# Second expert pass by seven products: the last sums of a chunk issued among the next chunk's products, a plain last chunk, three conversion steps per product

## The chip, the core and the metric

One NeuronCore of a Trainium2 chip runs the whole program. The metric is device time in microseconds (us) of one execution. The engines are TensorE (PE in the profile, PEld for its weight loads), VectorE (DVE), ScalarE (ACT), GpSimd (POOL) and the queue on SyncE (SP) that issues most transfers. Each engine takes its instructions in the order in which they were issued to it.

## What is computed

Attention with a decay mask on 4 x 8 heads of 576 positions, then two feed-forward layers on the 2304 tokens, all in float32:

```
ret = scores * Dmat            # scores = q k^T / sqrt(64), Dmat the decay mask
x   = ret @ v                  # as 2304 tokens x 512
r   = relu(x @ w_in);  x = (r * r) @ w_out                  # 512 -> 2048 -> 512
out = sum_e p[:, e] * (relu(x @ w1[e]) @ w2[e])             # 4 experts, 512 -> 1024 -> 512
```

## The kernel before

Every float32 operand of a product is split into a high part, rounded to the matmul's float32r format, and a low part, the rest; a product is then three matmuls (high by high, high by low, low by high) that add up in one PSUM bank. In the helper `split` (L129 to L131) ACT writes the high part and POOL subtracts it from the source for the low part.

The hidden width of both feed-forward layers is cut into chunks of 256: chunks 0 to 7 belong to the first layer, 8 to 23 to the four experts, and 24 to 39 are the experts' chunks once more. The tokens lie in five groups (four of 512, one of 256). Chunks 8 to 23, the first expert pass, serve groups 0, 1 and 4; chunks 24 to 39, the second expert pass, serve groups 2 and 3. The first pass converts the experts' weights (`split_w1`, `split_w2`: splits, and sums of weight blocks on DVE) in small steps. `tick(n)` issues the next n steps from a list, after every product of the pass; how many is in `pace`. `drain` issues what is left at once, where a chunk's weights must be ready. `keep` writes converted weights to DRAM after some empty steps, and `fetch` reads them back in the second pass through the SP queue, into one of two buffers per weight.

The second pass works on 2 x 2 blocks by Winograd's form of Strassen's scheme, in both layers: seven block products in place of eight, with sums of blocks around them. `first_layer(c)` is a generator with seven steps. Each issues one product of six matmuls (L791) into a PSUM bank and its sums: ACT copies the first bank to `u0` (L810), DVE adds (L798) and applies relu and the expert's probability (L801), POOL subtracts (L804). The results are seven operands for the second layer, each split by `operand`: "21", "22", "t3", "11", "t1", "t2", "t4". The last three are built on sums of the others: t1 = b12 - b11, t2 = b22 - t1, t4 = t2 - b21; all sources lie in the `spare_xh`/`spare_xl` tiles, t3 in a `wraw` tile. `second_layer(c)` takes the operands in the order 22, 21, t3, 11, t1, t2, t4: each step is two products of three matmuls (L860), and `gather` (L866 to L870) adds each bank to one of eight running sums e1 to e4, on DVE, or for the first chunk copies it there on ACT (L868). The main loop (from L1025) puts the steps of `first_layer(c)` and `second_layer(c - 1)` by turns, so a chunk is seven steps of twelve matmuls, 84 in all, for chunks 25 to 39. Order within each engine is the order of this code. The fourth step of `first_layer` adds a second product to the bank of the first, which `u0` must have been copied from by then.

The second layer of chunk 39 runs alone after the loop (`unit`, `second_layer(39)`): the last three operands are made there too, and as sums become final DVE combines them to the four output blocks (L904 to L906), `put` scales them by a stored factor on POOL, the last two on DVE (L933), and SP sends them out (L935).

Of the kernel before, what the change touches and what calls it, by code (L numbers as in the profile page):

```python
# [6 lines left out]
F32 = mybir.dt.float32  # L7
# [26 lines left out]
def tile_kernel(ctx, tc, qT, kT, kn, vn, v4d, mask, qdec, kdec, wd, w, probs, probs2, out, outT):  # L34
# [170 lines left out]
    def keep(f, c):  # L205

        for _ in range(3):
            yield
        for i, t in enumerate(w1t[c] if f is split_w1 else w2t[c]):
            d = dram.tile([128, 8 * BC], F32, name=f"kept{int(f is split_w2)}_{c}_{i}")  # L210
            nc.sync.dma_start(out=d, in_=f32(t))
            kept[f, c, i] = d

    def fetch(f, c):

        names = ("w2hi", "w2lo") if f is split_w2 else ("w1hi", "w1lo")
        parts = ((0, 1), (2, 8)) if f is split_w2 else ((0, 3), (4, 8))
        t = [wp.tile([128, 8 * BC], F32R, name=n) for n in names]
        for a, b in parts:
            for i in range(2):  # L220
                p = slice(BC * a, BC * b)
                nc.sync.dma_start(out=f32(t[i][:, p]), in_=kept[f, c - NW2, i][:, p])
        if f is split_w2:
            w2t[c] = t
        else:
            w1s[c] = [x.rearrange("p (i k m) -> p i k m", i=8, k=2) for x in t]
# [267 lines left out]
    with tc.manual_schedule():  # L494
# [260 lines left out]
        spare = []  # L755
        taken, ops, prow, sums = [0], {}, [], []

# [15 lines left out]
        def first_layer(c):  # L773
# [29 lines left out]
            def minus(o, x, y):  # L803
                g.tensor_tensor(out=o, in0=x, in1=y, op=ALU.subtract)  # L804
# [15 lines left out]
            product(b1, A12, 4, False)  # L820
            relu(b12, b1, 0)
            yield
            b5 = bank()
# [8 lines left out]
            o["22"] = operand(b22)  # L832
            minus(t3, b22, b12)
            o["t3"] = operand(t3)
            yield
# [3 lines left out]
            o["11"] = operand(b11)  # L839
            minus(b12, b12, b11)  # L840
            o["t1"] = operand(b12)
            minus(b22, b22, b12)
            o["t2"] = operand(b22)
            minus(b21, b22, b21)
            o["t4"] = operand(b21)
            yield

        def second_layer(c):
# [3 lines left out]
            o = ops.pop(c)  # L852
            first, last = c == NW1 + NW2, c == NW - 1
            bank = lambda: [ps.tile([128, GT], F32, name="h", tag="ps") for _ in range(2)]
# [11 lines left out]
            def gather(e, b, op=ALU.add, first=first):  # L866
                if first:
                    nc.scalar.copy(out=e, in_=b)  # L868
                else:
                    v.tensor_tensor(out=e, in0=e, in1=b, op=op)  # L870

            e1, e2, e3, e4 = ([t[:, 2 * i + d, :] for d in range(2)] for t in sums for i in range(2))
            bb = bank()
# [13 lines left out]
            for d in range(2):  # L887
                product(ba[d], H11, "11", False)
                gather(e1[d], ba[d])
                if last:  # L890
                    put(e1[d], 1, 0, d)
            yield
# [6 lines left out]
            for d in range(2):  # L899
                product(be[d], R2, "t2")  # L900
                gather(e2[d], be[d], first=False)
                if last:
                    c12, c22 = e2[d], e3[d]
                    v.tensor_tensor(out=c12, in0=e1[d], in1=e2[d], op=ALU.add)  # L904
                    v.tensor_tensor(out=c22, in0=c12, in1=e3[d], op=ALU.subtract)
                    v.tensor_tensor(out=e4[d], in0=c22, in1=e4[d], op=ALU.subtract)  # L906
                    put(c12, 0, 0, d)
                    put(c22, 0, 1, d)
            yield
            for d in range(2):  # L910
                product(bc[d], H22, "t4", False)
                if last:
                    v.tensor_tensor(out=e4[d], in0=e4[d], in1=bc[d], op=ALU.subtract)
                    put(e4[d], 1, 1, d, v)
                else:
                    gather(e4[d], bc[d])
            yield

        back = []

        def unit():
# [7 lines left out]
        def put(c, g, half, d, engine=nc.gpsimd):  # L929

            o = spare[put.n % 8] if engine is nc.gpsimd else c
            put.n += 1
            engine.tensor_tensor(out=o, in0=c, in1=back[g], op=ALU.mult)  # L933
            r = 256 * half + 128 * d
            nc.sync.dma_start(out=outT[r : r + 128, GT * g : GT * g + GT], in_=o)  # L935

        put.n = 0

# [25 lines left out]
        for i, job in enumerate(jobs):  # L964
# [4 lines left out]

            pace[0] = 4 if i < 3 else 3 if c in (p, q) else 4 if c == z else 2  # L970
            if job == (NW1, (0, 1)):
# [132 lines left out]
```

## Time and profile before

| | |
|---|---|
| median of 3 runs | 1382.35 us (1379.69 to 1383.57) |
| the profiled execution | 1382.66 us |
| its span, first to last instruction | 1380.9 us |
| PE busy | 1246.1 us, 90% |
| DVE, POOL, ACT busy | 901.4, 684.4, 442.9 us |
| mean granted TensorE clock | 0.952 of full speed |

The profile is one execution. Busy time is what an engine spent in instructions; matmuls overlap (a 128 x 512 matmul is shown with 0.39 us and the next starts 0.23 us after it), so the pace of PE is read from starts. The granted clock is 1.0 at 2.4 GHz and 0.5 at 1.2 GHz. By the timeline, the first pass of experts ends at about 918 us, the products of chunk 24 alone run to 939.81 us, the loop over chunks 25 to 39 to 1351.80 us, and the rest is the last second layer and the outputs.

### The profile page before, as it was taken

How to read it: one execution, taken by the hardware profiler on the slowest of the kernel's cores; microseconds unless marked ns; L12 is line 12 of the kernel's file. 1: busy time of each engine (PE TensorE's matmuls, PEld its weight loads, DVE VectorE, ACT ScalarE, POOL GpSimd, SP SyncE). 2: the span in 40 equal slices, each digit the busy share in tenths (PEclk: the TensorE clock that was granted, in tenths of full speed). 3: DMA queues.
4: the chain of work that ended last, by engine and by line, in shares of the span. 5: the costliest groups of instructions: out<-in, count | busy, mean ns of one | idle time of the engine just before them, and what ended most of it. 6: DMA issues, size and time to landing. Idle time of an engine off the chain costs nothing.

```text
span 1380.9 us, 18028 instructions
## 1 busy us (share of the span) xinstructions
PE 1246.1 (90%) x6464; PEld 1033.0 (75%) x6464; DVE 901.4 (65%) x1520; ACT 442.9 (32%) x1047; POOL 684.4 (50%) x702
## 2 busy tenths in 40 slices
PE   7999999999999999999999999877777887888684
PEld 6888888888888788878878788666656665666563
DVE  4776777877786846777767676754545554565457
ACT  4546333333333443433333333412111111111111
POOL 5655454545452535444543454504554465455547
PEclk9999999999999999999999999998898898899888
DMA  9911111111110144554545355564343344324421
GB/s 345 295 33 54 46 46 47 47 46 46 47 54 0 77 153 170 219 212 161 229 181 201 152 225 218 221 245 159 130 163 133 107 149 171 107 107 158 161 69 61
DMA packets 61277, 188.04 MB, mean 136 GB/s; under 512 B 7682, under 2 KB 12802, under 8 KB 52996
## 3 DMA queue, kind: packets, MB, share of 16 engines
q1 hardware_dynamic: 60676, 186.19, 37.3%
q8 instruction: 51, 0.84, 0.3%
q10 hardware_dynamic: 512, 0.70, 0.1%
q14 instruction: 38, 0.31, 0.1%
HBM read 115.02 MB, written 71.85 MB: 135 GB/s over the span
## 4 chain that ended last, share of the span: by engine, by line
PE 68%; POOL 15%; DVE 7%; ACT 5%; issue 3%; DMA 2%; SPq 0%; ACTq 0%; POOLq 0%; DVEq 0%
PE h L545 16%; PE o L740 14%; PE o L709 13%; PE h L579 11%; PE h L791 7%; PE h L860 5%; POOL glo L131 4%; POOL ghi L131 4%; POOL spare_xh L804 3%; POOL wraw L804 2%; ACT ghi L130 1%; POOL spare_xl L804 1%; ACT glo L130 1%; DVE xl L668 1%; PE qk L346 1%
## 5 line engine op out<-in xcount | busy, mean ns | idle before, releaser
L791 PE MATMUL h<-xh,w1hi 128*128 128x512 f32 x224 | 100.6, 449 | 83.0 <-ACT r L810 68.2
L131 POOL TENSOR_TENSOR glo<-r,ghi 128x512 fp32r<-128x512 f32 (+1 forms) x80 | 96.9, 1212 | 153.5 <-ACT ghi L130 143.3
L870 DVE TENSOR_TENSOR sums<-sums,h 128x512 f32<-128x512 f32 x214 | 139.6, 682 | 24.6 <-PE h L860 24.6
L545 PE MATMUL h<-xh,w1hi 128*128 128x512 f32 (+1 forms) x448 | 154.2, 344 | 0.8 <-DVE xl L433 0.8
L545 PE MATMUL h<-xl,w1hi 128*128 128x512 f32 (+1 forms) x448 | 154.1, 344 | 0.0
L545 PE MATMUL h<-xh,w1lo 128*128 128x512 f32 (+1 forms) x448 | 154.1, 344 | 0.0
L131 POOL TENSOR_TENSOR w2lo<-wraw,w2hi 128x256 fp32r<-128x256 f32 x64 | 52.2, 837 | 163.9 <-ACT w2hi L130 163.9
L740 PE MATMUL o<-w2lo,ghi 128*128 128x512 f32 x320 | 126.6, 395 | 4.5 <-POOL w2lo L131 4.5
L740 PE MATMUL o<-w2hi,ghi 128*128 128x512 f32 x320 | 126.5, 395 | 4.1 <-DVE oacc L748 3.0
L740 PE MATMUL o<-w2hi,glo 128*128 128x512 f32 x320 | 126.4, 395 | 0.0
L791 PEld LDWEIGHTS h<-xh,w1hi 128*128 128x128 f32 x224 | 47.8, 213 | 99.3 <-ACT r L810 73.6
L709 PE MATMUL o<-glo,w2hi 128*128 128x512 f32 (+1 forms) x320 | 118.2, 369 | 1.0 <-POOL glo L131 1.0
L709 PE MATMUL o<-ghi,w2hi 128*128 128x512 f32 (+1 forms) x320 | 118.0, 369 | 0.0
L709 PE MATMUL o<-ghi,w2lo 128*128 128x512 f32 (+1 forms) x320 | 117.8, 368 | 0.0
L748 DVE SCALAR_TENSOR_TENSOR oacc<-o,pr,oacc 128x512 f32<-128x512 f32 x150 | 107.6, 742 | 10.3 <-PE o L740 10.3
L798 DVE TENSOR_TENSOR r<-h,r 128x512 f32<-128x512 f32 x16 | 11.1, 692 | 153.3 <-ACT r L810 151.2
L550 DVE TENSOR_TENSOR r<-r 128x512 f32<-128x512 f32 (+1 forms) x80 | 62.4, 779 | 65.4 <-ACT r L549 65.1
L791 PE MATMUL h<-xl,w1hi 128*128 128x512 f32 x224 | 95.7, 427 | 0.0
L791 PE MATMUL h<-xh,w1lo 128*128 128x512 f32 x224 | 94.9, 424 | 0.0
L579 PE MATMUL h<-xh,w1hi 128*128 128x512 f32 x224 | 88.2, 394 | 6.6 <-ACT w1hi L130 5.0
L545 PEld LDWEIGHTS h<-xh,w1hi 128*128 128x128 f32 x448 | 84.9, 189 | 11.6 <-DVE xl L433 0.9
L545 PEld LDWEIGHTS h<-xl,w1hi 128*128 128x128 f32 x448 | 84.9, 189 | 10.6
(157 smaller groups left out, 3056.8 us busy)
## 6 DMA issues: line engine op xcount, KB each, us to landing
wraw<-wd SPq DMA_DIRECT2D x64, 256.0 KB, 2.8
wraw<-w SPq DMA_DIRECT2D x64, 256.0 KB, 3.0
kept<-w1hi SPq DMA_DIRECT2D x16, 1024.0 KB, 5.2
kept<-w1lo SPq DMA_DIRECT2D x16, 1024.0 KB, 7.1
kept<-w2hi SPq DMA_DIRECT2D x16, 1024.0 KB, 5.4
kept<-w2lo SPq DMA_DIRECT2D x16, 1024.0 KB, 6.3
w2hi<-kept SPq DMA_DIRECT2D x16, 768.0 KB, 5.1
w2lo<-kept SPq DMA_DIRECT2D x16, 768.0 KB, 6.2
```

The costliest lines, as they stand in the source:

```text
L130: nc.scalar.copy(out=hi, in_=src)
L131: nc.gpsimd.tensor_tensor(out=lo, in0=src, in1=f32(hi), op=ALU.subtract)
L545: nc.tensor.matmul(h, wk(a, f, k), group(x, g, k), start=(n == 0), stop=(n == 3 * KT - 1))
L550: nc.vector.tensor_tensor(out=r, in0=r, in1=r, op=ALU.mult)
L579: nc.tensor.matmul(o, a[:, i, k, :], slot(x, j)[:, k, :], start=(first and n == 0), stop=(n == 5), skip_group_check=True,)
L709: nc.tensor.matmul(o, a[:, f, 128 * m : 128 * m + 128], x[:, f, :], start=(n == 0), stop=(n == 3 * FT - 1))
L740: nc.tensor.matmul(o, a[:, f, 128 * m : 128 * m + 128], x[:, f, :], start=(n == 0), stop=(n == 3 * FT - 1))
L748: nc.vector.scalar_tensor_tensor(out=acc, in0=o, scalar=pr[:, tt, e : e + 1], in1=acc, op0=ALU.mult, op1=ALU.add)
L791: nc.tensor.matmul(o, a[:, i, k, :], slot(x, j)[:, k, :], start=(first and n == 0), stop=(n == 5), skip_group_check=True,)
L804: g.tensor_tensor(out=o, in0=x, in1=y, op=ALU.subtract)
L860: nc.tensor.matmul(b, a[:, BC * i + 128 * d : BC * i + 128 * d + 128], o[x][:, y, :], start=(first and n == 0), stop=(n == 2), skip_group_ ...
L870: v.tensor_tensor(out=e, in0=e, in1=b, op=op)
```

## The change

It has four parts.

1. In `first_layer` the operands t1, t2, t4 and the sums between them are no longer issued in the seventh step but put as four functions on a list `later`; the main loop takes one after each step of `first_layer`, before the step of `second_layer`. The seventh step fills the list before it yields, so the first function is issued at the end of that step and the other three in steps 1 to 3 of the next chunk.
2. The last chunk uses no seven products in its second layer: it makes operands "12", "21", "22", "11" alone, and `outputs` replaces `unit`, `put` and `second_layer(39)`. POOL combines the sums e1 to e4 to the four output blocks in six subtractions or additions, beside that 8 outputs of six matmuls are made, and DVE adds each to its block and scales it. Of the last w2, `fetch` reads the first four blocks alone.
3. `gather` copies the first chunk's banks on DVE, not on ACT.
4. `pace` is 3 rather than 2 in the first expert pass (4 in its last chunk as before), and `keep` waits one step rather than three.

```diff
     def keep(f, c):
-        for _ in range(3):
-            yield
+        yield
...
-        parts = ((0, 1), (2, 8)) if f is split_w2 else ((0, 3), (4, 8))
+        parts = ((0, 3), (4, 8))
+        if f is split_w2:
+            parts = ((0, 1), (2, 8)) if c < NW - 1 else ((0, 4),)
...
             relu(b12, b1, 0)
+            if c == NW - 1:
+                o["12"] = operand(b12)
...
-            minus(t3, b22, b12)
-            o["t3"] = operand(t3)
+            if c < NW - 1:
+                minus(t3, b22, b12)
+                o["t3"] = operand(t3)
...
             o["11"] = operand(b11)
-            minus(b12, b12, b11)
-            o["t1"] = operand(b12)
-            minus(b22, b22, b12)
-            o["t2"] = operand(b22)
-            minus(b21, b22, b21)
-            o["t4"] = operand(b21)
+            def one():
+                o["t1"] = operand(b12)
+                minus(b22, b22, b12)
+            def two():
+                o["t2"] = operand(b22)
+            def three():
+                minus(b21, b22, b21)
+            def four():
+                o["t4"] = operand(b21)
+            if c < NW - 1:
+                minus(b12, b12, b11)
+                later.extend((one, two, three, four))
             yield
...
                 if first:
-                    nc.scalar.copy(out=e, in_=b)
+                    v.tensor_copy(out=e, in_=b)
...
+        def outputs(c):
...
+            for a, b, op in ((e2, e1, ALU.add), (e3, e2, ALU.subtract), (e4, e3, ALU.subtract)):
+                for d in range(2):
+                    x, y = (a, b) if op == ALU.add else (b, a)
+                    nc.gpsimd.tensor_tensor(out=a[d], in0=x[d], in1=y[d], op=op)
+            for e, half, g, xs in (
+                (e1, 0, 1, ("11", "21")), (e2, 0, 0, ("12", "22")), (e3, 1, 0, ("12", "22")), (e4, 1, 1, ("11", "21"))
+            ):
+                for d in range(2):
...
+                    v.tensor_tensor(out=e[d], in0=e[d], in1=b, op=ALU.add)
+                    v.scalar_tensor_tensor(
+                        out=e[d], in0=e[d], scalar=1.0, in1=back[g], op0=ALU.mult, op1=ALU.mult
+                    )
+                    r = 256 * half + 128 * d
+                    nc.sync.dma_start(out=outT[r : r + 128, GT * g : GT * g + GT], in_=e[d])
...
-            pace[0] = 4 if i < 3 else 3 if c in (p, q) else 4 if c == z else 2
+            pace[0] = 4 if i < 3 else 3 if c in (p, q) else 4 if c == z else 3 if c >= NW1 else 2
...
-            for _ in zip(first_layer(c), second_layer(c - 1)):
-                pass
+            f, t = first_layer(c), second_layer(c - 1)
+            for _ in f:
+                if later:
+                    later.pop(0)()
+                next(t)
             queue_weights((split_w1, c + 2), (split_w2, c + 1))
-        unit()
-        for _ in second_layer(NW - 1):
-            pass
+        outputs(NW - 1)
```

On ACT, this is one chunk of the second pass before, from the copy of its first bank to that of the next chunk's. The first four casts are the high parts of 21, 22, t3 and 11, the next three those of t1, t2 and t4.

```order
L810 COPY r<-h 128x512
L130 CAST ghi<-spare_xh_9145 128x512
L130 CAST glo<-spare_xl_9146 128x512
L130 CAST ghi<-wraw 128x512
L130 CAST glo<-spare_xl_9146 128x512
L130 CAST ghi<-spare_xh_9145 128x512
L130 CAST glo<-spare_xl_9146 128x512
L130 CAST ghi<-spare_xh_9145 128x512
L810 COPY r<-h 128x512
```

And a chunk in the same tiles on ACT in the changed kernel, from the cast of 21 to that of t4:

```order
L130 CAST ghi<-spare_xh_9145 128x512
L130 CAST glo<-spare_xl_9146 128x512
L130 CAST ghi<-wraw 128x512
L130 CAST glo<-spare_xl_9146 128x512
L130 CAST ghi<-spare_xh_9145 128x512
L811 COPY r<-h 128x512
L130 CAST glo<-spare_xl_9146 128x512
L130 CAST ghi<-spare_xh_9145 128x512
```

The next chunk's copy has moved up past the casts of t2 and t4, and still stands behind the cast of t1. On POOL, DVE and PE the order within such a chunk is what it was.

On ACT ahead of chunk 23's first layer, the last chunk of the first pass, before (w1hi and w2hi are high parts of converted weights, L592 is ACT's copy of the first bank of a chunk, and the chunk's first product reads the first w1hi blocks):

```order
L130 CAST w2hi<-cv_d 128x256
L130 CAST w1hi<-wraw 128x256
L130 CAST w1hi<-cv_d 128x256
L130 CAST w1hi<-cv_m 128x256
L130 CAST w1hi<-wraw 128x256
L130 CAST w1hi<-cv_m 128x256
L130 CAST w1hi<-wraw 128x256
L130 CAST w1hi<-cv_d 128x256
L130 CAST w1hi<-wraw 128x256
L592 COPY r<-h 128x512
```

In the changed kernel, from chunk 22's copy to chunk 23's:

```order
L593 COPY r<-h 128x512
L562 ACTIVATE ghi<-h 128x512
L562 ACTIVATE ghi<-cv_tp 128x512
L562 ACTIVATE ghi<-r 128x512 x2
L593 COPY r<-h 128x512
```

The conversion of chunk 23's w1, and that of chunk 22's w2 ahead of it, no longer stands between the two chunks' first layers: with three steps a product it has been issued earlier.

## Rows read from the trace of the kernel before

**Rows 1.** The page: TensorE's busy time, and its granted clock in 40 slices.

```profile
PE 1246.1 (90%) x6464; PEld 1033.0 (75%) x6464; DVE 901.4 (65%) x1520; ACT 442.9 (32%) x1047; POOL 684.4 (50%) x702
...
PEclk9999999999999999999999999998898898899888
```

**Rows 2.** Waits of PE: line waited for, total us, times, longest us.

```profile
PE h L791 <- ACT r L810: 68.2, 13, 5.3
PE h L791 <- ACT sums L868: 7.9, 1, 7.9
...
PE h L579 <- ACT w1hi L130: 5.0, 1, 5.0
...
PE o L740 <- POOL w2lo L131: 4.5, 4, 1.4
```

**Rows 3.** Timeline, PE: start, us, line, operation, [idle before]. Loop's start, two waits, end.

```profile
939.81 0.39 PE L791 MATMUL h<-xh,w1hi 128*128 128x512 f32 x1
...
1119.61 0.79 PE L791 MATMUL h<-xh,w1hi 128*128 128x512 f32 x1 [5.25 <-ACT r L810]
...
1146.89 0.80 PE L791 MATMUL h<-xh,w1hi 128*128 128x512 f32 x1 [5.24 <-ACT r L810]
...
1351.80 0.39 PE L860 MATMUL h<-glo,w2hi 128*128 128x512 f32 x1
```

**Rows 4.** Timeline, PE: twelve matmuls apart before a wait, one apart after it.

```profile
1100.60 0.39 PE L791 MATMUL h<-xh,w1hi 128*128 128x512 f32 x1
...
1103.32 0.39 PE L791 MATMUL h<-xh,w1hi 128*128 128x512 f32 x1
...
1120.63 0.63 PE L791 MATMUL h<-xh,w1lo 128*128 128x512 f32 x1
...
1121.06 0.63 PE L791 MATMUL h<-xh,w1hi 128*128 128x512 f32 x1
```

**Rows 5.** Timeline, from the relu of 22 to the sum behind u0's copy.

```profile
1102.89 0.69 DVE L801 SCALAR_TENSOR_TENSOR spare_xl<-spare_xl,rows 128x512 f32<-128x512 f32 x1
...
1103.69 0.62 ACT L130 CAST ghi<-spare_xl 128x512 fp32r<-128x512 f32 x1 [2.20 <-DVE spare_xl L801]
...
1105.64 1.82 POOL L804 TENSOR_TENSOR wraw<-spare_xl,spare_xh 128x512 f32<-128x512 f32 x1
...
1110.69 1.29 POOL L804 TENSOR_TENSOR spare_xh<-spare_xh,spare_xl 128x512 f32<-128x512 f32 x1
...
1112.01 0.62 ACT L130 CAST glo<-spare_xh 128x512 fp32r<-128x512 f32 x1 [3.38 <-POOL spare_xh L804]
...
1118.46 0.62 ACT L130 CAST glo<-spare_xh 128x512 fp32r<-128x512 f32 x1 [2.59 <-POOL spare_xh L804]
...
1118.98 0.58 ACT L810 COPY r<-h 128x512 f32<-128x512 f32 x1
...
1119.59 0.69 DVE L798 TENSOR_TENSOR r<-h,r 128x512 f32<-128x512 f32 x1 [9.94 <-ACT r L810]
```

**Rows 6.** Timeline, DVE: first sum of 22, and two steps after the wait.

```profile
1102.16 0.69 DVE L798 TENSOR_TENSOR spare_xl<-h,r 128x512 f32<-128x512 f32 x1
...
1120.20 1.27 DVE L870 TENSOR_TENSOR sums<-sums,h 128x512 f32<-128x512 f32 x2
...
1121.39 0.69 DVE L798 TENSOR_TENSOR spare_xh<-h,r 128x512 f32<-128x512 f32 x1
```

**Rows 7.** Windows, one chunk: PE, PEld, DVE, ACT, POOL busy, clock, DMA share, GB/s.

```profile
1118.40:1145.90 27.50, 22.04 (x84) 17.65 (x84) 14.75 (x23) 4.89 (x9) 14.43 (x12) 0.88 0.40 145
```

**Rows 8.** A chunk's last fetch, in SP's timeline, and such fetches' median time to landing.

```profile
1110.62 0.61 SPq L222 DMA_DIRECT2D w1lo<-kept  x1
...
w1lo<-kept SPq DMA_DIRECT2D x15, 512.0 KB, 8.9
```

**Rows 9.** Timeline, last scalings: two on POOL, one on DVE.

```profile
1373.02 3.38 POOL L933 TENSOR_TENSOR spare_xh<-sums,wraw 128x512 f32<-128x512 f32 x2
...
1375.90 1.04 DVE L933 TENSOR_TENSOR sums<-sums,wraw 128x512 f32<-128x512 f32 x1
```

More of the change, by code (lines that the diff above doesn't have):

```diff
@@ L755, in tile_kernel @@
         spare = []
-        taken, ops, prow, sums = [0], {}, [], []
+        taken, ops, prow, sums, later = [0], {}, [], [], []
         def operand(src):
@@ L852, in second_layer @@
             o = ops.pop(c)
-            first, last = c == NW1 + NW2, c == NW - 1
+            first = c == NW1 + NW2
             bank = lambda: [ps.tile([128, GT], F32, name="h", tag="ps") for _ in range(2)]
@@ L867, in gather @@
                 if first:
-                    nc.scalar.copy(out=e, in_=b)
+                    v.tensor_copy(out=e, in_=b)
                 else:
                     v.tensor_tensor(out=e, in0=e, in1=b, op=op)
-            e1, e2, e3, e4 = ([t[:, 2 * i + d, :] for d in range(2)] for t in sums for i in range(2))
+            e1, e2, e3, e4 = totals()
             bb = bank()
@@ L889, in second_layer @@
                 gather(e1[d], ba[d])
-                if last:
-                    put(e1[d], 1, 0, d)
             yield
@@ L901, in second_layer @@
                 gather(e2[d], be[d], first=False)
[L902 to L908, printed above, removed]
             yield
@@ L911, in second_layer, with totals @@
                 product(bc[d], H22, "t4", False)
[L912 to L916, printed above, removed]
-            yield
-        back = []
-        def unit():
+                gather(e4[d], bc[d])
+            yield
+        def totals():
+            return ([t[:, 2 * i + d, :] for d in range(2)] for t in sums for i in range(2))
+        def outputs(c):
+            w2h, w2l = w2t[c]
+            o = ops.pop(c)
+            v = nc.vector
+            back = []
             for i in range(2):
@@ L927, in unit @@
                 back.append(t)
[L929 to L937, printed above, removed]
+            e1, e2, e3, e4 = totals()
+            for a, b, op in ((e2, e1, ALU.add), (e3, e2, ALU.subtract), (e4, e3, ALU.subtract)):
[6 more added lines that the diff above has]
+                for d in range(2):
+                    b = ps.tile([128, GT], F32, name="h", tag="ps")
+                    n = 0
+                    for f in range(2):
+                        i = (H11, H12)[f] + half
+                        for a, y in ((w2h, 0), (w2h, 1), (w2l, 0)):
+                            nc.tensor.matmul(
+                                b, a[:, BC * i + 128 * d : BC * i + 128 * d + 128], o[xs[f]][:, y, :],
+                                start=(n == 0), stop=(n == 5),
+                            )
+                            n += 1
+                    v.tensor_tensor(out=e[d], in0=e[d], in1=b, op=ALU.add)
+                    v.scalar_tensor_tensor(
+                        out=e[d], in0=e[d], scalar=1.0, in1=back[g], op0=ALU.mult, op1=ALU.mult
+                    )
+                    r = 256 * half + 128 * d
+                    nc.sync.dma_start(out=outT[r : r + 128, GT * g : GT * g + GT], in_=e[d])
         def layer2(job):
```

## The prediction

> **What bounds the kernel now.** I read the page first. TensorE is busy for 90% of the span, and its clock is granted in full from start to the 27th of 40 slices, then 8 to 9 tenths [rows 1]. So the first two thirds have little to give, and the last third, the second expert pass, loses both time and clock. The waits of PE say where: 68.2 us in 13 waits of the first-layer products for ACT's copy `u0`, and one of 7.9 us for ACT's first-chunk copies; all others are smaller [rows 2].
>
> Then the timeline. The wait recurs every 1146.89 - 1119.61 = 27.28 us [rows 3]. Twelve matmuls take 1103.32 - 1100.60 = 2.72 us, 0.2267 us each [rows 4], so the 84 of a chunk need 19.04 us. The wait itself is 5.24 us. The remaining 3.0 us is the clock: after the wait matmuls start 0.43 us apart [rows 4], at the 1.2 GHz level, and over a chunk the grant is 0.88 [rows 7]. The loop lasts 1351.80 - 939.81 = 411.99 us [rows 3] where 15 chunks at 2.4 GHz would need 285.6: it loses 126.4 us. It is PE's wait on one in-order queue. DVE is busy for 14.75 us of a chunk and POOL for 14.43 [rows 7], and neither would fill 19.04.
>
> Why the copy is late stands in the timeline from the relu of 22 [rows 5]. POOL's sums alternate with ACT's casts: t3's subtraction at 1105.64, t1's at 1110.69, its cast at 1112.01, t4's cast at 1118.46, and only then the copy, at 1118.98. Its bank had been full since the chunk's first product; the chunk began at 1119.61 - 5.25 - 36 x 0.2267 = 1106.20.
>
> **Part 1, the deferred sums.** By the order on ACT, the copy now stands behind t1's cast and no longer behind those of t2 and t4. Behind a cast it started 0.52 us after it [rows 5], so it would start at 1112.53, 6.45 us earlier. That is more than the 5.24 us of waiting: the wait goes, with 1.2 us to spare.
>
> What is late next? A closed chain remains, from the sum behind `u0` through DVE's queue to operand 22, through POOL and ACT to t1's cast, and to the next `u0`. DVE, running behind, needs 1121.39 - 1119.59 = 1.80 us a step [rows 5, 6] for three steps; then a step with a sum and a relu, 0.73 from sum to relu, 0.61 from there to the next, and 1.80 - 0.61 = 1.19 for the two gathers [rows 5, 6], 2.53; then 22's sum and relu, 0.73 + 0.69. That is 9.35 us. From the end of that relu, 1103.58, to t1's cast, 1112.01, are 8.43, to the copy 0.52 and to the sum behind it 0.61 [rows 5]: 9.56 us. The chain is 18.91 us against PE's 19.04. PE keeps the lead by a hair.
>
> The hair can go. In the rows POOL did most subtractions while DVE stood still. Beside a relu of two SBUF inputs a subtraction took 1.82 us, else 1.29 [rows 5], 0.53 more; that one is in the chain already. Two further relus, of 21 and 22, may now meet POOL: 18.91 + 0.53 = 19.44 or 18.91 + 1.06 = 19.97. I take 19.24, between none (19.04) and one, because the tie is so close; ends 19.04 and 19.97. Fifteen chunks: 288.6 us, a **gain of 123.4** (112.4 to 126.4). In the Trainium skill, the page "SBUF — State Buffer", section "SBUF: two separate sides", states more: a VectorE op with two SBUF inputs and a GpSimd op that reads SBUF exclude each other, and whichever comes second blocks until the first has finished. By that a relu could cost a whole POOL op twice a chunk; the 0.53 of the row agrees with it in kind, and the case is rival A.
>
> The deferred operands come in time. t1's cast stood 1112.01 - 1106.20 = 5.8 us after the chunk's start, t4's cast 6.45 later, and a low part is done some 2.0 after its cast's start: 22's lies between its cast at 1103.69 and t3's subtraction at 1105.64 [rows 5]. So t4 is ready at 14.3, and its products start at 6.5 x 2.72 = 17.7. Fetches: a chunk's last weight transfer is issued at 1110.62, 4.4 after the start, and lands 8.9 later [rows 8], at 13.3; the shorter chunk needs it at 19.04. With no wait left, the clock should be granted as in the first 27 slices [rows 1].
>
> **Part 2, the last chunk.** From 1351.80 to the span's end, 1380.9, are 29.1 us. Now PE has 48 matmuls, 10.9 us, after a wait for the low part of 11. By the pattern of 22 that ends 3.5 us after its first sum began (1102.16 to the cast at 1103.69, and 2.0 more) [rows 5, 6]; 11's sum begins some 1.1 us before the loop's end, so PE starts in earnest at 2.4, and DVE with the first output at 3.9. DVE has an addition and a scaling for each of eight outputs: 0.73 + 0.61 = 1.34 us alone, or 0.73 + 1.04 = 1.77 when POOL works beside it [rows 6, 9], as it does: six sums at up to 1.69 each [rows 9], 10.1 us. So DVE ends at 14.6 to 18.1. The last scaling before ended at 1376.94 and the span 3.96 later [rows 9]. The tail is 18.6 to 22.1; I take 21, since POOL is busy for most of it: **gain 8.1** (7.0 to 10.5).
>
> **Part 3, the first chunk's copies** cost DVE what eight other gathers do; the waits they caused are within the 126.4. Nothing more.
>
> **Part 4, the conversions.** A first-pass chunk has 12 products that tick. At two steps that is 24 for 30 steps of work (two conversions of 12, two `keep` of 3), at three it is 36 for 26. So the drains find nothing left, as the order ahead of chunk 23 shows. PE's waits there were 5.0 us for w1hi and 4.5 for w2lo [rows 2], and after the long one some 3.0 of clock as in the loop: 12.5 us at most. Work hides the rest, and PE's pace is unchanged. What is added: a conversion's first DVE sum may now wait for its raw tile, since `keep` leaves one step instead of three; queued behind are the accumulations that free PE's banks. Eight banks hold eight outputs of six matmuls, 10.9 us, and even the slow fetch of the rows lands in 8.9 [rows 8]. I take a **gain of 12** (0 to 12.5).
>
> **Sum**, against the profiled execution of 1382.66 us (its span and 1.76 around it; the median of the runs, 1382.35, is 0.3 less): 1382.66 - 123.4 - 8.1 - 12 = **1239**. With all ends: 1233 to 1263.
>
> **Rival A, DVE and POOL block each other.** If both relus wait for a whole POOL op of 1.29 [rows 5], the chain is 18.91 + 2.58 = 21.5 us and bounds: 15 x 2.25 = 34 more, 1273. For it: the margin of 0.13. Against: one row shows 0.53, not 1.29. Chance 0.10.
>
> **Rival B, the copy stays late.** It still stands behind a cast that waits for POOL. If POOL, now busy in another rhythm, brings t1's cast more than the 1.2 us later, the wait comes back there, and the change does only half of what it says: a chunk midway between 19.2 and 27.3, 23.2, gives 1298. Chance 0.05.
>
> **Rival C, the conversions get in the way.** Three steps after each product can put w1 casts ahead of a chunk's copy on ACT as in the 5.0 us wait; at 8 us with its clock, in half of 14 chunks, + 56 and no gain of 12: 1307. The order ahead of chunk 23 speaks against. Chance 0.05.
>
> **Rival D, slower: the clock stays low.** If the tight chain leaves many short waits, in steps 5 to 7, the clock may fall again and again. A chunk with a share f of its matmuls at 0.43 us costs 19.24 + 17.1 f [rows 4]; 143 us, the forecast's whole gain, are 9.6 a chunk, so the kernel turns slower above f = 0.56, and at 0.65 it is 1239 + 15 x 11.1 = 1406. Against: in the matmuls before each wait PE changes bank every three or six matmuls, at full pace [rows 4]. Chance 0.02. The Trainium skill, "TensorE: Matmul & The Clock Gate", section "A second HAM failure mode: psum-queue depth-cycling", tells of a kernel whose small idle times between matmul groups, as it cycled through banks, made the clock go up and down; by that rule this would happen, and the rows just named do not show it.
>
> **Numbers.** Forecast 0.78, A 0.10, B 0.05, C 0.05, D 0.02. Its own range is 1233 to 1263; 3 us more on either side, for parts 2 and 4, give 1230 to 1266, which leaves out the rivals, some 0.2. A measurement here tells 0.3%, about 4 us, from no change. All but D are faster: 0.97, slower 0.02, same 0.01.
>
> **What would show it.** Right: products of chunks 25 to 39 recur every 19.0 to 20.0 us, the waits for L811's copy are gone, the clock is full through the second pass, the span ends some 21 us after the last chunk's loop, and the waits for w1hi and w2lo are gone. Wrong: a new wait of PE in each chunk of over 1 us, relus or POOL sums stretched to twice their time, waits of pairs' first products in the first pass.

## The result, and the profile after

The changed kernel takes **1244.07 us** (median of 4 runs, 1242.9 to 1247.13) beside 1381.64 for the kernel before in the same session: a ratio of 0.9008, 95% interval 0.8987 to 0.9029. The forecast was 1239.0 us, with a range of 1230 to 1266. The profiled execution took 1243.94 us; its span is 1242.0 us, 138.9 shorter than before.

Lines from L205 on have moved: `first_layer`'s products are now at L792, its sums at L799, relus at L802, subtractions at L805, the copy `u0` at L811; the second layer's products are at L875, `gather`'s sums at L885. The new `outputs` has POOL's sums at L939, PE's products at L949, DVE's additions and scalings at L954 and L955.

The page, against [rows 1]:

```profile
PE 1202.4 (97%) x6470; PEld 1006.1 (81%) x6470; DVE 897.5 (72%) x1522; ACT 435.3 (35%) x1036; POOL 681.6 (55%) x695
...
PEclk9999999999999999999999999999989999999999
```

TensorE is busy for 97% instead of 90%, in fewer microseconds, because the clock is now full in the last third too: one slice stands at 8, around chunk 24, where PE still waits 6.9 us for a sum of DVE, which itself waits for the probabilities (`rows`).

Waits of PE, against [rows 2] (line waited for, total us, times, longest us):

```profile
PE h L792 <- DVE spare_xh L799: 6.9, 1, 6.9
...
PE h L580 <- ACT r L593: 3.9, 3, 2.1
PE h L580 <- DVE cv_tp L587: 3.7, 3, 1.9
...
PE h L949 <- ACT glo L130: 2.2, 1, 2.2
```

The wait for `u0`'s copy, 68.2 us in 13 waits, is not in the list any more, nor is that for ACT's first-chunk copies. The two waits at L580 belong to the first pass; in the stretch measured below four of the six are new.

Timeline of PE, against [rows 3]: the loop's start, the end of one chunk and the first product that the copy releases, the loop's last product, and the first two products behind it.

```profile
933.15 0.39 PE L792 MATMUL h<-xh,w1hi 128*128 128x512 f32 x1
...
1055.34 0.39 PE L875 MATMUL h<-glo,w2lo 128*128 128x512 f32 x1
1055.60 0.50 PE L792 MATMUL h<-xh,w1hi 128*128 128x512 f32 x1
1055.94 0.39 PE L792 MATMUL h<-xl,w1hi 128*128 128x512 f32 x1
...
1220.50 0.39 PE L875 MATMUL h<-glo,w2lo 128*128 128x512 f32 x1
1223.14 0.49 PE L949 MATMUL h<-glo,w2hi 128*128 128x512 f32 x1 [2.25 <-ACT glo L130]
1224.49 0.67 PE L949 MATMUL h<-glo,w2hi 128*128 128x512 f32 x1 [0.86 <-POOL glo L131]
```

The last product starts at 1220.50 and the next could start 0.23 later, so the loop ends at 1220.73.

Windows of the loop and of the tail, with the columns of [rows 7]:

```profile
1220.73:1242.00 21.27, 13.22 (x49) 10.08 (x48) 14.27 (x20) 1.67 (x3) 11.16 (x8) 0.91 0.26 99
933.15:1220.73 287.58, 287.58 (x1261) 235.57 (x1259) 219.88 (x343) 71.65 (x121) 223.05 (x165) 1.00 0.53 187
```

The 138.7 us between the two profiled executions lie in these stages. The first pass is measured between two marks that both traces have: the end of PE's 0.75 us wait near 480 us, and the end of its wait of some 6.9 us in chunk 24.

| stage | before, us | after, us | difference | forecast |
|---|---|---|---|---|
| loop, chunks 25 to 39 | 411.99 | 287.58 | -124.4 | -123.4 |
| tail | 29.10 | 21.27 | -7.8 | -8.1 |
| first expert pass | 454.27 (479.48 to 933.75) | 446.36 (480.66 to 927.02) | -7.9 | -12 |
| ahead of 480 us, chunk 24's rest, around the span | | | +1.4 | 0 |

Of the last row 1.2 us lie ahead of the first pass, in work that the change does not touch; that stage ended between 478.69 and 482.03 us in the profiles of this study, so it is the spread from one execution to the next. The total lies some 5 us above the forecast, and 4 of these are the first pass.

### The profile page after: what moved, and what is told of

It reads as the page before. It is cut to its first block, busy times and chain, and to the rows that moved or that the text cites. A ratio compares the mean times of both kernels' runs of the same rounds, so it can differ in the third digit from the quotient of the medians.

```text
span 1242.0 us, 18075 instructions
## 1 busy us (share of the span) xinstructions
PE 1202.4 (97%) x6470; PEld 1006.1 (81%) x6470; DVE 897.5 (72%) x1522; ACT 435.3 (35%) x1036; POOL 681.6 (55%) x695
## 4 chain that ended last, share of the span: by engine, by line
PE 81%; DVE 9%; DMA 3%; ACT 2%; issue 2%; POOL 1%; SPq 0%; ACTq 0%; DVEq 0%; POOLq 0%
PE h L546 18%; PE o L741 14%; PE o L710 14%; PE h L792 11%; PE h L875 11%; PE h L580 10%; DMA wraw<-w 2%; DVE xl L669 1%; PE qk L347 1%; DVE y L637 1%; DMA k_n<-kn 1%; DMA rows<-rows 1%; PE xo L399 1%; DVE y L676 1%; DVE oacc L749 1%
## 5 line engine op out<-in xcount | busy, mean ns | idle before, releaser
L885 DVE TENSOR_TENSOR sums<-sums,h 128x512 f32<-128x512 f32 x202 | 128.5, 678 | 1.9 <-PE h L875 1.9
L580 PE MATMUL h<-xh,w1hi 128*128 128x512 f32 x224 | 88.6, 396 | 7.6 <-ACT r L593 3.9
L792 PE MATMUL h<-xh,w1hi 128*128 128x512 f32 x224 | 88.8, 397 | 6.9 <-DVE spare_xh L799 6.9
L546 PEld LDWEIGHTS h<-xh,w1hi 128*128 128x128 f32 x448 | 84.9, 189 | 11.7 <-DVE xl L434 0.9
L546 PEld LDWEIGHTS h<-xh,w1lo 128*128 128x128 f32 x448 | 84.8, 189 | 10.1
L718 DVE TENSOR_TENSOR y<-o,y 128x512 f32<-128x512 f32 (+1 forms) x140 | 86.2, 628 | 3.8 <-PE o L710 3.6
L580 PE MATMUL h<-xl,w1hi 128*128 128x512 f32 x224 | 87.9, 393 | 0.0
L580 PE MATMUL h<-xh,w1lo 128*128 128x512 f32 x224 | 87.7, 392 | 0.0
```

Source lines behind the costliest of these rows:

```text
L546: nc.tensor.matmul(h, wk(a, f, k), group(x, g, k), start=(n == 0), stop=(n == 3 * KT - 1))
L580: nc.tensor.matmul(o, a[:, i, k, :], slot(x, j)[:, k, :], start=(first and n == 0), stop=(n == 5), skip_group_check=True,)
L718: nc.vector.tensor_tensor(out=y, in0=o, in1=y, op=ALU.add)
L792: nc.tensor.matmul(o, a[:, i, k, :], slot(x, j)[:, k, :], start=(first and n == 0), stop=(n == 5), skip_group_check=True,)
```

## The experiments

**1. The copy ahead of t1's cast.** The forecast put the chunk at 19.24 us because a closed chain of 18.91 or more competes with PE's 19.04. If so, the copy must come sooner once it no longer waits for t1's cast. All four deferred functions are issued one step later:

```diff
             f, t = first_layer(c), second_layer(c - 1)
+            due = len(later)
             for _ in f:
-                if later:
+                if due:
                     later.pop(0)()
+                due = len(later)
                 next(t)
```

> The changed kernel with the first of the four deferred functions also issued one step later, so that on ScalarE the next chunk's first copy stands ahead of the cast of t1 too; nothing else moves. The changed kernel's chunks recur every 19.26 us, 0.22 above the 19.04 of 84 matmuls, and its PE starts the second product of the first bank 0.05 us after that copy ends. Theory (the closed chain through the copy sets the pace, 18.91 worked out plus one relu of 1.13 us in place of 0.69 in it): with the copy out of the chain the chunks recur every 19.04 us, the copy lies some 3 us earlier, the loop over chunks 25 to 39 falls from 287.6 to about 285 us, and the whole by 2 to 3 us from 1244; the relu of 22 stays stretched, at no cost. Rival (PE itself, or VectorE and GpSimd blocking each other, sets 19.26): the period stays at 19.2 to 19.3 and the time at 1244.

Measured: 1242.01 us (1240.39 to 1244.76), ratio to before 0.8981 (0.8964 to 0.8999). The median's 2.1 us alone could not be told from no change; the trace can tell it. Window of the loop in this kernel:

```profile
933.15:1218.76 285.61, 285.61 (x1261) 236.30 (x1259) 229.86 (x343) 71.77 (x121) 220.62 (x166) 1.00 0.53 188
```

and its timeline around a copy, on ACT and on PE:

```profile
1049.53 0.62 ACT L130 CAST ghi<-spare_xl 128x512 fp32r<-128x512 f32 x1
1050.05 0.58 ACT L811 COPY r<-h 128x512 f32<-128x512 f32 x1
...
1050.11 0.39 PE L792 MATMUL h<-xh,w1hi 128*128 128x512 f32 x1
```

The loop is 285.61 us, the 285.6 that 15 x 84 matmuls need. In the changed kernel it is 287.58, and there the product behind the copy starts 0.05 us after the copy's end (1054.97 + 0.58 = 1055.55; 1055.60 above), 0.26 after the product ahead of it and 0.34 before the next, where 0.23 is the pace. So the chain through POOL and ACT sets the changed kernel's period, by 0.22 us a chunk, and with the copy off that chain PE sets it. It does so only from the seventh chunk of the loop on: by the starts of their first products, chunks 25 to 30 still last 19.04 us, while PE uses up its lead, and the later ones 19.23 to 19.28. That is why the loop gains 2.0 us and not 15 x 0.22 = 3.3.

The tail, with the same code, is 19.84 us here and 21.27 in the changed kernel. At its start PE waits 1.62 us instead of 2.25, and its granted clock stays at 1.00 from 1220.53 to 1232.00, where the changed kernel has 0.50 from 1224.90 to 1228.00. No forecast had this.

**2. All four functions at the end of the seventh step**, as in the kernel before, with the rest of the change kept:

```diff
-                later.extend((one, two, three, four))
+                for make in (one, two, three, four):
+                    make()
```

> The changed kernel with the three last operands made at the end of a chunk's seventh step again, all ahead of the next chunk's copy on ScalarE; the plain last chunk, the first chunk's copies on VectorE and the three conversion steps stay. Theory (the place of the copy is worth 8 us a chunk): PE waits 5.2 us for it in each chunk again, its clock falls after each wait and chunks recur every 27.3 us; over 14 or 15 chunks that is 113 to 121 us, so 1357 to 1365 us. Rival (the other parts carry a good share of the gain in the loop, say the first chunk's copies): under 1340 us.

Measured: 1360.55 us (1359.15 to 1360.76), ratio 0.9834 (0.9817 to 0.985). Waits of PE, and two of them in its timeline:

```profile
PE h L792 <- ACT r L811: 77.4, 15, 5.3
```

```profile
1134.74 0.80 PE L792 MATMUL h<-xh,w1hi 128*128 128x512 f32 x1 [5.27 <-ACT r L811]
...
1162.02 0.79 PE L792 MATMUL h<-xh,w1hi 128*128 128x512 f32 x1 [5.25 <-ACT r L811]
```

The old wait is back in full, in all 15 chunks, 27.28 us apart as in [rows 3]. The order of these casts alone is worth 1360.55 - 1244.07 = 116.5 us here; what the other parts give without it is 1383.66 - 1360.55 = 23.1 us (1383.66 is the kernel before in the same session).

**3 to 5. The two edits on conversions**, each taken back and each alone. The changed kernel has three steps per product and one empty step in `keep`.

Both as before:

```diff
-        yield
+        for _ in range(3):
+            yield
...
-            pace[0] = 4 if i < 3 else 3 if c in (p, q) else 4 if c == z else 3 if c >= NW1 else 2
+            pace[0] = 4 if i < 3 else 3 if c in (p, q) else 4 if c == z else 2
```

> The changed kernel with two conversion steps per product in the first expert pass and three empty steps ahead of the writing to DRAM, as before; all else changed. From the copy of chunk 8's pair to that of chunk 24 the kernel before takes 440.65 us and the changed one 432.74. Theory (the conversions give 7.9 us net: 10.6 us of waits and their clock go, 6.1 us of new short waits come): this stage is 440 to 441 us, PE waits 5 us for w1hi ahead of chunk 23 and 1.4 us for w2lo three or four times, and the whole is 1251 to 1253 us. Rival (the gain in that stage comes from elsewhere, such as transfers): the stage stays near 433 and the whole at 1244 to 1246.

Three steps per product, `keep` as before:

```diff
-        yield
+        for _ in range(3):
+            yield
```

> The changed kernel with three empty steps ahead of the writing to DRAM as before, but three conversion steps per product. Theory (the four new PE waits of the first pass, 6.1 us in all, come from VectorE standing in its queue for a raw weight tile whose load was issued only a step earlier, 40.4 us in 15 waits against 8.1 before): with two more steps between, those VectorE waits fall to under 30 us, the PE waits to under 3 us, the stage from chunk 8's pair to chunk 24 from 432.7 to 428 to 431 us. Rival (the new waits are made by the three steps a product alone, whatever keep does): PE waits of 5 to 7 us stay and the stage is 432 to 434.

Two steps per product, `keep` as changed:

```diff
-            pace[0] = 4 if i < 3 else 3 if c in (p, q) else 4 if c == z else 3 if c >= NW1 else 2
+            pace[0] = 4 if i < 3 else 3 if c in (p, q) else 4 if c == z else 2
```

> Of the conversions' two edits one alone: two steps per product as before, but the writing back of a converted weight takes one step instead of three. The stretch from chunk 8's pair wait to chunk 24's first copy was 440.7 us before, 432.7 in the changed kernel, 428.2 with three steps and the old writing back. Theory (the short writing back makes the next conversion begin before its raw tile has come, and the three steps do the gain): 24 steps for 26 of work leave a small drain, PE waits 1 to 4 us for w1hi or w2, DVE waits less for raw tiles than the changed kernel's 40 us since the pace is slower; the stretch is 434 to 440 us, in all 1246 to 1251 us. Rival (the short writing back did the gain and the three steps cost it the waits for raw tiles): the stretch is 427 to 431 us, 1239 to 1243 us.

Measured, with the first pass between the two marks of the stage table, and DVE's waits for raw tiles (`cv_m L167 <- DMA wraw<-w`, the first sum of a w1 conversion):

The profiles of the second and the last row are the slowest and the fastest of their four executions. The expectations measure the pass between two copies (440.65 us before, 432.74 in the changed kernel), which gives the same difference of 7.9.

| steps, empty steps in `keep` | median, us | ratio to before | first pass, us | DVE's waits, us (times) |
|---|---|---|---|---|
| 2, 3 (kernel before) | 1381.64 | 1 | 454.27 | 8.1 (8) |
| 2, 3 (rest changed) | 1251.79 | 0.9055 (0.9036 to 0.9074) | 456.21 | 9.3 (10) |
| 2, 1 | 1245.92 | 0.9014 (0.8995 to 0.9033) | 447.58 | 35.3 (15) |
| 3, 1 (changed kernel) | 1244.07 | 0.9008 (0.8987 to 0.9029) | 446.36 | 40.4 (15) |
| 3, 3 | 1241.57 | 0.8971 (0.8951 to 0.8991) | 441.60 | 24.9 (13) |

With both edits taken back the median is 7.7 us longer, as the theory had it. Three steps alone take 12.7 us off the pass (10.7 in the longest of the three profiles named below): what the forecast had taken for both edits. One empty step alone takes 6.7 off, so either edit does much of the work, and beside three steps it gives 4.8 back. Its total, 1245.92, lies a hair under the theory's 1246 to 1251 and far from the rival's. In the medians the 2.5 us between the last two rows can't be told from nothing, and two kernels whose first pass is the same (the first two rows) differ by 1.9 us in this stretch. The other profiles settle it: with three steps and three empty ones the pass is 441.60, 442.58 and 443.57 us (experiments 4, 9 and 10); with three steps and one it is 446.35 to 446.97 in the changed kernel and experiments 1, 2, 6 and 8, and 450.32 in experiment 7.

Waits of PE in the kernel with two steps and one empty step, those of the first pass:

```profile
PE h L580 <- ACT w1hi L130: 3.6, 1, 3.6
...
PE o L741 <- POOL w2lo L131: 2.2, 2, 1.4
...
PE h L580 <- POOL w1lo L131: 1.1, 1, 1.1
```

These are the waits of [rows 2] for weights that are not ready, smaller but not gone; with three steps and the old `keep` none is among the waits listed. So the short `keep` shrinks the old waits by about a third, from 10.6 us (these two and one of 1.1 for w2hi) to 6.9, and the three steps remove them. What the short `keep` costs is in the changed kernel's own timeline, in the section on the reasons.

**6. First chunk's copies on ACT again**

```diff
-                    v.tensor_copy(out=e, in_=b)
+                    nc.scalar.copy(out=e, in_=b)
```

> One part of the change alone undone: the first chunk's sums are copied out of their banks by ACT again, eight copies, instead of by DVE. My theory (a chunk's copy u0 is the last link of a closed chain and ACT's queue is in order): the eight copies join ACT's queue between casts that wait for POOL, so PE waits for them once, in chunk 25 alone, 2 to 8 us; chunks 26 to 39 keep the changed kernel's spacing of 19.26 us; in all 1246 to 1253 us against 1244.1. Rival (the copies were late only because the casts of t2 and t4 stood ahead, which they no longer do): no wait, 1243 to 1245 us.

Measured: 1247.7 us (1246.23 to 1248.86), ratio 0.9028 (0.9005 to 0.9052). Timeline of ACT at the start of chunk 26, and of PE:

```profile
958.95 0.62 ACT L130 CAST ghi<-spare_xh 128x512 fp32r<-128x512 f32 x1 [3.37 <-POOL spare_xh L805]
959.47 1.07 ACT L883 COPY sums<-h 128x512 f32<-128x512 f32 x2
960.43 0.60 ACT L811 COPY r<-h 128x512 f32<-128x512 f32 x1
...
960.10 0.50 PE L792 MATMUL h<-xh,w1hi 128*128 128x512 f32 x1 [1.50 <-ACT sums L883]
```

PE waits once, 1.50 us, below the 2 to 8 expected, and in chunk 26 rather than 25: two of the eight copies stand between t1's cast and the next `u0`. The loop (933.96 to 1223.01) is 289.05 us, 1.5 longer. The rest of the 3.4 us by which the span is longer lies outside of it: 1.1 in the tail, the others ahead of the loop, and nothing in the edit explains these. So the moved copies are worth 1.5 us that the trace shows, where the kernel before had PE wait 7.9 us for such copies in the first layer [rows 2] and 5.7 in the second. Most of those waits came with the old order of the casts, and not with the copies alone.

**7. The last chunk by seven products again**, all else as changed (the functions `unit`, `put` and the last branch of `second_layer` as before, in place of `outputs`):

```diff
-            parts = ((0, 1), (2, 8)) if c < NW - 1 else ((0, 4),)
+            parts = ((0, 1), (2, 8))
...
-        outputs(NW - 1)
+        while later:
+            later.pop(0)()
+        unit()
+        for _ in second_layer(NW - 1):
+            pass
```

> One part of the change alone undone: the last chunk goes by seven products as before (its sums and splits after the loop, outputs by POOL from the gathered sums), all else as changed. Theory (the tail of before was 29.1 us and part 2 of the prediction takes 8.1 off it): the tail comes back at 28 to 30 us, and the loop, whose last chunk now has its late operands issued behind it, stays within 2 us; in all 1250 to 1253 us. Rival (the gain of the last chunk came from the copies and casts that no longer wait, not from the plain products): the tail is 22 to 25 us, 1245 to 1248 us.

Measured: 1253.65 us (1252.73 to 1255.71), ratio 0.9073 (0.9053 to 0.9094). The loop (935.94 to 1223.61) is 287.67 us, as in the changed kernel; the tail, to the span's end at 1253.9, is 30.3. So the plain last chunk is worth 9.0 us here, and the theory stands, with total and tail a little above the expected ranges.

**8. The outputs in another order.** In the changed kernel the profile puts the wait of DVE's first addition down to POOL, in the timeline of both:

```profile
1224.39 2.51 POOL L939 TENSOR_TENSOR sums<-sums 128x512 f32<-128x512 f32 x2
...
1226.97 0.69 DVE L954 TENSOR_TENSOR sums<-sums,h 128x512 f32<-128x512 f32 x1 [3.42 <-POOL sums L939]
...
1238.40 0.69 DVE L955 SCALAR_TENSOR_TENSOR sums<-sums,wraw 128x512 f32<-128x512 f32 x1
```

The addition writes e1 in place, which POOL's first sum must have read. But it also needs its bank from PE, whose last product for it starts at 1226.24 and takes 0.63 us, so the bank is full at about 1226.87. The same code of the end in the kernel with two steps and one empty step tells the two apart; there DVE starts while POOL is in its second sum, and the profile names PE:

```profile
1226.89 2.52 POOL L939 TENSOR_TENSOR sums<-sums 128x512 f32<-128x512 f32 x2
...
1228.57 0.69 DVE L954 TENSOR_TENSOR sums<-sums,h 128x512 f32<-128x512 f32 x1 [2.52 <-PE h L949]
```

So the first output is held by its own products, which need the low part of 11, and not by POOL, as the expectation below takes it. The experiment starts with e2, whose products need operands 12 and 22 alone, writes to spare tiles, and issues one POOL sum ahead of the low part of 11:

```diff
-                (e1, 0, 1, ("11", "21")), (e2, 0, 0, ("12", "22")), (e3, 1, 0, ("12", "22")), (e4, 1, 1, ("11", "21"))
+                (e2, 0, 0, ("12", "22")), (e1, 0, 1, ("11", "21")), (e3, 1, 0, ("12", "22")), (e4, 1, 1, ("11", "21"))
...
-                    v.tensor_tensor(out=e[d], in0=e[d], in1=b, op=ALU.add)
+                    to = spare[(4 * (c % 2) + 4 + made[0]) % 8]
+                    v.tensor_tensor(out=to, in0=e[d], in1=b, op=ALU.add)
...
+                if c == NW - 1 and "22" in ops[c] and "11" not in ops[c]:
+                    combine(1)
```

> The end alone is changed: the outputs are made in the order of the sums that need least, one of POOL's six closing sums is issued ahead of the low part of 11, and the results go to spare tiles, so that DVE need not wait for POOL to have read a sum. Theory (DVE's first output was held 3.4 us by POOL's sums, and DVE's sixteen steps then set the end): DVE begins 3 to 3.5 us earlier, the tail is 18 us instead of 21.3, in all 1240 to 1242 us. Rival (DVE and POOL exclude each other, so that DVE pays with longer steps for each of POOL's sums that it no longer waits for): DVE's steps beside POOL stretch from 0.7 to over 1.3 us, the tail stays 20.5 to 21.5, 1243 to 1245 us.

Measured: 1242.67 us (1238.9 to 1244.07), ratio 0.8987 (0.8964 to 0.9011). Timeline of POOL and DVE in this kernel, whose loop ends at 1221.27 and whose span ends at 1240.8:

```profile
1222.35 1.75 POOL L935 TENSOR_TENSOR sums<-sums 128x512 f32<-128x512 f32 x1
...
1225.30 1.74 POOL L935 TENSOR_TENSOR sums<-sums 128x512 f32<-128x512 f32 x1
...
1224.13 0.69 DVE L968 TENSOR_TENSOR spare_xh<-sums,h 128x512 f32<-128x512 f32 x1
...
1227.07 0.69 DVE L968 TENSOR_TENSOR spare_xh<-sums,h 128x512 f32<-128x512 f32 x1 [1.18 <-POOL sums L935]
1227.79 1.05 DVE L969 SCALAR_TENSOR_TENSOR spare_xh<-spare_xh,wraw 128x512 f32<-128x512 f32 x1
```

DVE begins 2.86 us after the loop's end instead of 6.24, 3.4 earlier, as the theory said but not for its reason: PE's first products no longer need 11 and follow the loop without a wait. The tail gains half of that, 19.5 for 21.27 us: the second addition waits 1.18 us for POOL's second sum, and five scalings beside POOL take 0.96 to 1.07 us, where in the changed kernel three take over 0.9. The tail lies between the two expectations, and in the medians the 1.4 us can't be told from nothing; DVE's start was not the whole of the tail.

**9 and 10. The three that gained, together**, and the same with `combine(2)` in place of `combine(1)`.

> The three edits that each gained something, together: the deferred functions one step later, three steps a product with the old writing back, the reordered outputs. By the stages of the profiles the loop gives 2.0 us (285.6 instead of 287.6), the first pass 4.5 to 4.8, the tail 1.7: if these lie in stages that follow one another they add, 8.2 to 8.5 us, 1235 to 1237 us. Rival (they overlap: a shorter stage only makes the next wait for its transfers): as far as the medians of the single runs go, 2.1 + 2.5 + 1.4 = 6 us or less, 1238 us or more.

> The same, but two of POOL's six closing sums instead of one ahead of the low part of 11. Theory (DVE's second output waits 1.2 us for the second sum): that wait goes and the tail is 0.8 to 1.2 us shorter. Rival (DVE beside POOL is slowed by what POOL has to read, whenever it reads): DVE's scalings stretch to 1.0 for as long as POOL works, and the tail is within 0.4 us of the other's; the totals cannot be told apart either way (0.3% is 4 us), so the trace decides.

Measured: 1235.89 us (1233.76 to 1238.28), ratio 0.8939 (0.8923 to 0.8955), and 1236.05 us (1235.08 to 1237.37), ratio 0.8939 (0.8926 to 0.8953). Windows of the first one's loop and tail:

```profile
929.38:1214.98 285.60, 285.60 (x1261) 236.49 (x1260) 230.01 (x343) 71.80 (x121) 220.76 (x166) 1.00 0.53 188
1214.98:1233.90 18.92, 11.35 (x49) 8.74 (x47) 14.38 (x20) 1.68 (x3) 11.49 (x8) 0.92 0.30 111
```

The first pass is 442.58 us (480.99 to 923.57). Against the changed kernel that is 2.0 in the loop, 2.3 in the tail and 3.8 in the pass: they add, and the intervals of the two ratios (0.8923 to 0.8955, and 0.8987 to 0.9029) don't meet. This version beats both kernels.

With two sums first, the wait of 1.18 us is gone, but the low part of 11 comes later and PE waits for it; behind that wait TensorE's clock is granted at 0.53 from 1219.10 to 1222.70. The waits of PE in this kernel, and DVE's third addition:

```profile
PE h L962 <- POOL glo L131: 2.1, 1, 2.1
```

```profile
1221.06 0.69 DVE L969 TENSOR_TENSOR spare_xl<-sums,h 128x512 f32<-128x512 f32 x1 [1.79 <-PE h L962]
```

The tail is 1233.3 - 1213.59 = 19.7 us, 0.8 longer. Neither theory said so: POOL's queue is full there, and what is put ahead in it is paid for behind.

## Why the prediction was right, point by point

**Part 1 was right in size and in mechanism.** The chunk was taken at 19.24 us and is 19.26 (copies at 1035.71, 1054.97 and 1074.23); PE itself recurs at this pace from chunk 31 on. The closed chain is there, step by step. From the sum behind one `u0` (1036.33) to the end of 22's relu (1046.09) are 9.76 us, where 9.35 had been worked out; from there to the next such sum at 1055.58 are 9.49 for 9.56. Timeline of the changed kernel on POOL, DVE and ACT, with the copy that answers to [rows 5]:

```profile
1042.45 1.83 POOL L131 TENSOR_TENSOR ghi<-spare_xh,ghi 128x512 fp32r<-128x512 f32 x1 [0.73 <-ACT ghi L130]
1044.24 1.30 POOL L131 TENSOR_TENSOR glo<-spare_xh,glo 128x512 fp32r<-128x512 f32 x1
...
1042.43 0.69 DVE L802 SCALAR_TENSOR_TENSOR spare_xh<-spare_xh,rows 128x512 f32<-128x512 f32 x1
...
1044.96 1.13 DVE L802 SCALAR_TENSOR_TENSOR spare_xl<-spare_xl,rows 128x512 f32<-128x512 f32 x1
...
1055.58 0.69 DVE L799 TENSOR_TENSOR r<-h,r 128x512 f32<-128x512 f32 x1 [4.45 <-ACT r L811]
...
1054.44 0.62 ACT L130 CAST glo<-spare_xh 128x512 fp32r<-128x512 f32 x1 [3.38 <-POOL spare_xh L805]
1054.97 0.58 ACT L811 COPY r<-h 128x512 f32<-128x512 f32 x1
```

22's relu met POOL's low part of 21 and took 1.13 us instead of 0.69. These 0.44 us are all that the first part of the chain is longer than worked out, and nearly the 0.53 that the forecast had for one such meeting. That 19.24 came so near was partly luck: it was a middle between no meeting and one, a whole meeting came, the second part of the chain was 0.07 shorter, and the early chunks, at 19.04, weren't in the sum. Experiment 1 shows that this chain, and not PE, sets the period: with the copy off it the loop falls to PE's own 285.6.

**Rival A** asked what a meeting of DVE and POOL costs. The Trainium skill, "SBUF — State Buffer", section "SBUF: two separate sides", says that the later of the two blocks until the earlier has finished. The rows agree: the relu issued at 1044.96 ends 0.55 us after POOL's op ends (1045.54), and POOL's low part of 1.83 us ends 1.16 after the relu that began at 1042.43 ended (1043.12), where 1.30 is its usual time. But a meeting costs what is left of the earlier op, 0.44 to 0.53 us in these rows, and not the 1.29 that the rival took for each; only one was on the chain, and the chunk came out at 19.26, not 21.5. It can cost more where the two start together: in the tail of the kernel with two steps and one empty step a scaling of 0.69 us, from 1229.36 on, takes 1.84 beside a POOL sum from 1229.37 on.

**Rivals B and D** did not come, and rival C in small. The copy waits for t1's cast, but PE by only 0.22 us. In the first pass w1 casts did stand ahead of a copy, for 2.09 us of PE's time at most (below), and not 8. The clock was granted in full over all of the loop's 287.58 us. The Trainium skill, "TensorE: Matmul & The Clock Gate", section "A second HAM failure mode: psum-queue depth-cycling", would have it go up and down with small idle times between groups; with a bank change every three or six matmuls and a gap of some 0.2 us in each later chunk the loop's trace does not show it, at a granted clock of 1.00.

**Part 2 was right in size by errors that cancel**, which is luck. The forecast's 2.4 us was for the products on the low part of 11, and the first of these starts 3.76 us after the loop's end (1224.49); what starts at 2.41 (1223.14) is one product on the high part. The forecast had the sum of 11 begin 1.1 us before the loop's end, and it begins 0.18 before it, at 1220.55. Then came the 1.2 GHz level, so the first bank was full at about 1226.87, and DVE's first output came at 6.24, not 3.9. From there DVE took 12.12 us to its end at 18.36 (1239.09), where the 21 holds some 13.1; and from there to the span's end were 2.9 us, not 3.96. The sum, 21.27, met the forecast's 21.

**Part 3, "nothing more"**, holds to 1.5 us in the trace of experiment 6.

**Part 4 is the step that was mis-sized**: 12 us forecast, 7.9 measured (its range was 0 to 12.5). Both waits named, for w1hi and w2lo, are gone. What came instead stands in the timeline of the changed kernel's first pass, on DVE, ACT and PE:

```profile
513.01 0.42 DVE L167 TENSOR_TENSOR cv_m<-wraw 128x256 f32<-128x256 f32 x1 [5.38 <-DMA wraw<-w]
...
515.40 0.50 PE L580 MATMUL h<-xh,w1hi 128*128 128x512 f32 x1 [1.94 <-DVE cv_tp L587]
...
536.15 0.42 DVE L167 TENSOR_TENSOR cv_m<-wraw 128x256 f32<-128x256 f32 x1 [3.26 <-DMA wraw<-w]
...
537.13 0.41 ACT L130 CAST w1hi<-cv_d 128x256 fp32r<-128x256 f32 x1 [4.15 <-DVE cv_d L167]
...
540.50 0.57 ACT L593 COPY r<-h 128x512 f32<-128x512 f32 x1
...
541.13 0.50 PE L580 MATMUL h<-xh,w1hi 128*128 128x512 f32 x1 [2.09 <-ACT r L593]
```

The forecast had named this wait (a conversion's first sum, for its raw tile) and set it at nothing, because eight banks cover it. That argument failed: PE did not run out of banks. It waited for one bank to be read, because the pair's next product is added to what stands in that bank: at 515.40 for the sum that DVE takes from it, queued behind the waiting one, and at 541.13 for ACT's copy, queued behind casts that wait for DVE's conversion sums. The four new waits of PE (1.94, 2.09, 1.07 and 0.96) make 6.1 us in the stretch, and behind that of 2.09 the clock is granted at 0.58 from 542.20 to 546.00, some 1.6 us more, an estimate from that grant. With three empty steps in `keep` DVE's waits fall from 40.4 to 24.9 us, the new waits of PE to 2.9 (1.43 and 1.48), and the pass is 4.8 us shorter. That the load itself comes late because its tile is freed only by the conversion before it was not tried (a fourth raw tile would tell).

## What to carry to other kernels

When a wait is taken away by moving work in an in-order queue, follow the chain that remains through all the queues until it closes on itself, and compare its length with the bound engine's period: here 19.26 against 19.04 us, and one more move of the same kind won the rest. Cover against a wait is not only free buffers: ask which one buffer must be read, by an instruction that stands behind the waiting one, before the bound engine can go on. And a faster issue of side work pays as long as its inputs have come; cutting the slack between two conversions made the next one stand in the queue and wait there.

## What was not expected of the hardware

TensorE's clock fell behind waits of 2.1 to 2.3 us in these kernels, and not always at once. Ahead of the plain last chunk PE waits 2.25 us in the changed kernel, and 0.86 once more behind one product; there the matmuls that follow from 1224.96 on start 0.43 us apart, at the 1.2 GHz level, until about 1228. In the kernel with two steps and one empty step the waits are 2.24 and 0.85 us; the first matmuls behind them start at the pace of 2.4 GHz, but from 1228.26 on, about a microsecond later, they are 0.43 us apart as well (0.53 granted from 1228.20 to 1231.80). PE's timeline, changed kernel and then that one:

```profile
1224.96 0.63 PE L949 MATMUL h<-glo,w2lo 128*128 128x512 f32 x1
1225.38 1.05 PE L949 MATMUL h<-glo,w2hi 128*128 128x512 f32 x2
```

```profile
1227.32 0.39 PE L949 MATMUL h<-glo,w2lo 128*128 128x512 f32 x1
...
1228.26 1.05 PE L949 MATMUL h<-glo,w2hi 128*128 128x512 f32 x2
```

Behind the wait of 1.62 us at the same place in experiment 1, and behind that of 1.94 us in the first pass of the changed kernel, the clock stayed full; behind those of 5.25 us in [rows 3, 4] it fell. What decides stays open.
